# A causal long convolution with a gated feed-forward on one core: block 2's spectrum by n mod 4, two product sums by accumulating transfers, and a new order of the work

## The chip, the cores and the metric

One Trainium2 chip, one of its cores. The metric is device time in microseconds of one execution, from inputs in HBM to the output in HBM; the times given are medians of several runs. The core's engines are named as in the profile: PE (TensorE) multiplies matrices, DVE (VectorE) and ACT (ScalarE) work on elements, POOL (GpSimd) does small element work and issues transfers, SP only issues transfers. Each takes its own instructions strictly in order and waits where a semaphore makes it wait.

## The reference

For one sequence of 2048 positions with 640 channels (A_q, A_k, A_v are 2048 x 640):

```python
k_shift = sum(k_pad[:, t:t+S] * shift_k[:, 3-t] for t in range(4))   # causal filter of 4 taps along the sequence
kv = k_shift * v
y  = irfft(rfft(pad(kv)) * rfft(pad(ssm_k)))[:S]                     # causal convolution over all 2048 positions, by channel
y  = y + kv * ssm_D
h  = x + layernorm(x) * y                                            # x = A_q
h2 = h + (silu(layernorm(h) @ w_gate) * (layernorm(h) @ w_up)) @ w_down   # 640 -> 1728 -> 640
```

Inputs and output are bfloat16. B_x is not used.

## The kernel before

**Blocks.** The sequence is cut into four blocks of 512 positions. A block lies as 128 partitions x 4 residues r = n mod 4 x 640 channels. Block j of the convolution needs inputs 0 to j with kernel slices j to 0: each input block and each slice gets a spectrum of its own once, the products are summed over the pairs, and one inverse transform gives the block. The transform is an odd-frequency DFT of length 1024, done as matmuls with constant matrices: `WF` forward, `WI` inverse. A spectrum is a tile `S` of two halves in frequency, each with two cosine and two sine rows of 640 channels (128 x 2560 elements a half).

**Stages of block j**, with the names that the code gives its steps: loads (`Lg`, `Lk`, `Lv`, `Lx`); `g`: the kernel slice turned; `G`: its spectrum; `h`: windows of neighbouring slices; `k`: the 4-tap filter on PE and the product with v; `X`: the spectrum of the input; `m0`..`m3`: products of spectra; `n`: sums for the first layernorm; `i`: inverse transform, h and the sums of the second layernorm; `t`: layernorm of h, turned for the feed-forward; `f`: the feed-forward (13.5 chunks of 128 gate and up columns, then the down projection). The feed-forward of block j - 1 runs on PE among the convolution steps of block j; that of block 3 has nothing left beside it.

**Order.** The program first writes down all steps as a plan, each with an engine, what it reads and writes, and the buffers it holds. `ORDER` is a list of the plan's numbers, written out by hand or by a tool: the program is issued in that order, so each engine's queue is the list filtered by its engine. A negative number ~n takes step n's second form: an eviction from PSUM or an application of a layernorm on DVE in place of ACT, or a weight load issued by POOL in place of SP. Buffers (12 of `big`, 8 of `S`, 4 of PSUM and so on) go in turn to the steps as they come in the list; a step that takes a buffer waits for the last user of it.

**Spectrum, two forms** (`transform`, L391). In the form "sub" each of the four basis rows is summed by PE over residues 0 and 2, evicted doubled, then over 1 and 3 on top, evicted; DVE's one difference of full half-size (128 x 2560) gives the second half of the frequencies. In the form "four" PE sums each of the cosine and sine rows over one residue, then over a second, for even and for odd residues:

```python
forward(src, 2 * sin, rs[:1], ps, ws, True, False, [odd, dst])
taken(ps, tmp[1], tmp[0], ws, True)
forward(src, 2 * sin, rs[1:], ps, ws, False, True, [odd, dst])
taken(ps, a[1], a[0], ws)
```

DVE then makes one difference of 128 x 1280 for the even and one for the odd residues, `hi4` (full size) is the upper half, and the lower half is a sum that, for the names in `ADDLO` ('G1', 'G2', 'X1', 'X2', 'X3'), is not made by DVE: `add_into` (L276 to L279) lets POOL issue a transfer from SBUF to SBUF that adds to its target. `SUM` names the transforms that take the form "four".

**Products** (`mac`, L707). For each pair of spectra after the first, four steps: a product (L746) and its sum into `A` (L747) on DVE. Where the pair of parts stands in `ADDP` under (block, input), the step is a product alone (L741), and the sum into `A` is an accumulating transfer by `add_into`. The products of block 3 with inputs 1 and 2 are the steps `m1`, `m2` of that block.

**Inverse** (`inverse`, L813). In the form "four" (blocks 2 and 3) DVE makes two half-size steps for the even residues (L843) and two for the odd ones (L858); then PE makes one product for each residue (L878). The sum of A's halves ahead of it is an accumulating transfer in block 2. POOL makes the scale of the second layernorm in blocks 1 and 2 (`norm`, L760 to L791).

Of the kernel before, what the change touches and what calls it, by code (L numbers as in the profile page):

```python
# [46 lines left out]
SUM = {'X3': 'four', 'i2': 'four', 'i3': 'four', 'G3': 'four'}  # L47
ADDP = {(1, 1): ((0, 1),)}
# [164 lines left out]
def kernel(ctx: ExitStack, tc: tile.TileContext, A_q, A_k, A_v, A_shift_k, A_ssm_k, A_ssm_D, B_x,  # L213
# [165 lines left out]
    def wide(n, ws):  # L379
        return n if len(ws) == 2 else n // 2 + 75  # L380
# [10 lines left out]
    def transform(src, dst, pieces, minus=None, name=None):  # L391

        how = SUM.get(name, "sub")
        for ws in pieces:
# [418 lines left out]
    def inverse(A, x, n1, pieces=((0, 1),), minus=None, groups=(ROWS,)):  # L813
# [4 lines left out]
        for ws in pieces:  # L818
            if not minus:
# [10 lines left out]
                else:  # L830
                    dve(wide(1490, ws), low, [], [(A, bits(ws=ws))])
            four = not minus and SUM.get(f"i{plan.block}") == "four"
            if four:
# [404 lines left out]
    for j in range(1, NB):  # L1238
# [25 lines left out]
        if last:  # L1264
            A = H[j]
            stage("m0")
            mac(A, X[0], H[j], True, at=(j, 0), adds=ADDP.get((j, 0), ()))
        stage("k")
# [62 lines left out]
```

## Time and profile before

| | |
|---|---|
| time, median of 3 runs | 260.67 us (260.61 to 261.63) |
| the profiled execution's own time | 261.3 us |
| its span, first to last instruction | 259.6 us |
| PE busy | 251.3 us (97%) |
| DVE busy | 198.6 us (77%) |
| ACT busy | 180.0 us (69%) |
| POOL busy | 97.0 us (37%) |
| DMA | 45.38 MB, mean 175 GB/s |

Times in the profile are microseconds from the span's start, or ns where a column says mean of one. A busy share is an average over the whole span; the stages have different limits, so the table of stretches says more. In a row of a timeline stand start, duration, engine, line of the kernel, operation, target <- sources, and in brackets how long the engine sat idle before it and what ended that. Matmuls overlap in PE's pipeline, so the duration of one (299 ns at 320 columns) is longer than the distance to the next.

### The profile page before, as it was taken

What the parts mean: (1) busy time and instruction counts of PE and PEld (TensorE: products, weight loads), DVE (VectorE), ACT (ScalarE), POOL (GpSimd) and SP (SyncE); (2) the same over time, 40 slices, a digit from 0 to 9 for tenths busy, and PEclk for the clock granted to TensorE, in tenths of its full rate; (3) what the DMA queues carried; (4) which work ended last, traced back from release to release, by engine and by line L of the source; (5) the groups of instructions that cost most, each with busy time, mean ns of one, the idle gap of its engine ahead of it and who ended that gap; (6) DMA issues with size and microseconds to landing.
All of it is one profiled execution on the core that took longest, in us unless ns stands there. A gap on an engine that the chain in (4) does not pass through costs nothing.

```text
span 259.6 us, 4700 instructions
## 1 busy us (share of the span) xinstructions
PE 251.3 (97%) x1803; PEld 154.2 (59%) x1818; DVE 198.6 (77%) x259; ACT 180.0 (69%) x297; POOL 97.0 (37%) x115
## 2 busy tenths in 40 slices
PE   8999899999998999999999999999999999999994
PEld 7967577654654477754465477544456764444663
DVE  4679999999998999999999999999998200004403
ACT  2899999999998998569855985655497134637200
POOL 7961300008914199926117962240951022000000
PEclk9999999999999999999999999999999999999999
DMA  6997999979999998999997965994498546000002
GB/s 218 403 251 119 289 252 340 280 115 279 247 238 168 182 217 204 190 191 201 214 231 110 299 151 107 198 238 130 100 215 255 101 77 70 8 0 0 13 15 76
DMA packets 64752, 45.38 MB, mean 175 GB/s; under 512 B 31014, under 2 KB 60267, under 8 KB 64731
## 3 DMA queue, kind: packets, MB, share of 16 engines
q1 hardware_dynamic: 58896, 32.96, 51.1%
q0 software_dynamic: 5824, 12.13, 24.9%
q8 instruction: 14, 0.23, 0.4%
q14 instruction: 8, 0.06, 0.1%
q10 hardware_dynamic: 10, 0.01, 0.0%
HBM read 30.01 MB, written 4.59 MB: 133 GB/s over the span
## 4 chain that ended last, share of the span: by engine, by line
PE 78%; ACT 9%; DMA 6%; DVE 2%; issue 2%; SPq 1%; ACTq 0%; DVEq 0%
PE ps L1022 40%; PE ps L1110 23%; PE ps L375 10%; DMA big<-in_B_w_up_dram 4%; PE ps L878 3%; DMA big<-in_A_q_dram 3%; ACT T L565 2%; ACT big L364 1%; ACT S L364 1%; PE ps L648 1%; ACT row L757 1%; ACT big L664 1%; ACT big L473 1%; ACT tT L1014 1%; DVE row L892 1%
## 5 line engine op out<-in xcount | busy, mean ns | idle before, releaser
L1022 PE MATMUL ps<-big,big 128*128 128x512 bf16 x525 | 119.9, 379 | 1.7 <-DMA big<-in_B_w_up_dram 0.8
L1022 PEld LDWEIGHTS <-big 128*128 128x128 bf16 x540 | 52.5, 98 | 61.1 <-DMA big<-in_B_w_up_dram 1.3
L1110 PE MATMUL ps<-wd,tT 128*128 128x320 bf16 (+1 forms) x416 | 60.3, 299 | 0.0
L1110 PEld LDWEIGHTS <-tT 128*128 128x128 bf16 x416 | 40.7, 98 | 16.3
L1016 DVE TENSOR_TENSOR tT<-tT,co 128x2048 bf16<-128x2048 bf16 x12 | 14.5, 1219 | 34.4 <-ACT tT L1014 32.4
L375 PE MATMUL ps<-big,WF 128*128 128x320 bf16 x240 | 39.1, 299 | 1.3 <-ACT big L364 1.0
L1012 ACT CAST co<-ps 128x1024 bf16<-128x1024 f32 x24 | 24.2, 1011 | 17.3 <-PE ps L1022 16.8
L747 DVE TENSOR_TENSOR S<-S,big 128x2560 bf16<-128x2560 bf16 x23 | 34.3, 1492 | 1.2 <-DMA S<-big 0.5
L746 DVE TENSOR_TENSOR big<-S,S 128x2560 bf16<-128x2560 bf16 x23 | 34.1, 1485 | 0.2
L375 PEld LDWEIGHTS <-WF 128*128 128x128 bf16 x240 | 23.1, 97 | 12.8 <-issue 2.3
L1014 ACT ACTIVATE tT<-ps 128x1024 bf16<-128x1024 f32 x24 | 24.5, 1029 | 8.8 <-PE ps L1022 8.7
L757 ACT ACTIVATE row<-big 128x640 bf16<-128x640 bf16 x32 | 23.5, 742 | 1.8 <-DMA big<-in_A_q_dram 1.1
L807 ACT ACTIVATE row<-big,sm 128x640 bf16<-128x640 bf16 x23 | 20.3, 922 | 3.8 <-POOL sm L789 2.8
L1117 POOL DMA_DIRECT2D out_dram<-row x12 | 11.8, 1010 | 29.2 <-ACT row L1116 29.1
L364 ACT CAST S<-ps 128x320 bf16<-128x320 f32 (+1 forms) x36 | 19.4, 583 | 0.3
L1116 ACT CAST row<-ps 128x640 bf16<-128x640 f32 x12 | 8.1, 691 | 14.2 <-PE ps L1110 13.2
L364 ACT ACTIVATE big<-ps 128x640 bf16<-128x640 f32 (+1 forms) x24 | 15.6, 696 | 0.7 <-PE ps L375 0.7
L278 POOL DMA_DIRECT2D big<-row x8 | 7.0, 919 | 22.9 <-DVE row L892 22.9
L892 DVE SCALAR_TENSOR_TENSOR row<-row,ps 128x640 bf16<-128x640 bf16 x16 | 12.8, 815 | 1.1 <-PE ps L878 0.9
L278 POOL DMA_DIRECT2D S<-big x2 | 2.5, 1266 | 26.3 <-DVE S L719 19.1
L719 DVE TENSOR_TENSOR big<-S,S 128x2560 bf16<-128x2560 bf16 (+1 forms) x10 | 12.2, 1218 | 0.1
L959 POOL DMA_DIRECT2D big<-in_B_w_gate_dram x8 | 9.1, 1137 | 8.1 <-PE ps L1022 7.8
(110 smaller groups left out, 330.4 us busy)
## 6 DMA issues: line engine op xcount, KB each, us to landing
big<-in_B_w_up_dram SPq DMA_DIRECT2D x17, 320.0 KB, 5.1
big<-in_B_w_gate_dram SPq DMA_DIRECT2D x16, 320.0 KB, 4.7
big<-in_A_ssm_k_dram SPq DMA_DIRECT2D x4, 640.0 KB, 9.2
big<-in_A_q_dram SPq DMA_DIRECT2D x4, 640.0 KB, 7.6
big<-in_A_v_dram SPq DMA_DIRECT2D x4, 640.0 KB, 6.9
big<-in_B_w_gate_dram POOLq DMA_DIRECT2D x8, 320.0 KB, 7.2
big<-in_B_w_up_dram POOLq DMA_DIRECT2D x7, 320.0 KB, 6.7
wd<-in_B_w_down_dram SPq DMA_DIRECT2D x1, 2080.0 KB, 12.2
```

The costliest lines, as they stand in the source:

```text
L364: (lambda: nc.scalar.activation(dst(), src(), ACT.Copy, scale=2.0)) if twice else (lambda: nc.scalar.copy(dst(), src())),
L375: nc.tensor.matmul(ap(ps)[:, h, 0:NH], w, ap(src)[:, r, h * NH:(h + 1) * NH], start=(first and i == 0), stop=(last and i == len(rs) - 1), ...
L746: nc.vector.tensor_mul(flat2(b), X.part(xs), H.part(hs))
L747: f(A.part(dst), A.part(dst), flat2(b))
L757: act(825, lambda r=r, junk=junk: nc.scalar.activation(ap(junk), ap(x)[:, r, :], ACT.Square, scale=D ** -0.5, accum_out=sm(s, 1)[:, r:r + ...
L807: nc.scalar.activation(ap(row), ap(x)[:, r, :], ACT.Identity, bias=sm(s, 5)[:, r:r + 1], scale=sm(s, 4)[:, r:r + 1])
L892: nc.vector.scalar_tensor_tensor(two(ap(t)), two(ap(t)), 1.0, half(ap(ps)), op0=ALU.mult, op1=ALU.mult, accum_out=sm(s, 0)[:, r:r + 1])
L1012: act(1010, lambda ps=ps: nc.scalar.copy(ap(co)[:, at:at + 2, :], ap(ps)), src, [(co, gi % 2)])
L1014: act(1010, lambda ps=ps: nc.scalar.activation(ap(tT)[:, c:c + 2, :], ap(ps), ACT.Silu), src, [done(range(c, c + 2), ROWS)])
L1016: dve(1220, lambda: nc.vector.tensor_mul(ap(tT)[:, c - 2:c + 2, :], ap(tT)[:, c - 2:c + 2, :], ap(co)), [co], [done(range(c - 2, c + 2), R ...
L1022: nc.tensor.matmul(ap(ps)[:, i, :], ap(w)[:, k, off:off + P], ap(hT)[:, k, :], start=(k == 0), stop=(k == KT - 1))
L1110: nc.tensor.matmul(ap(ps)[:, hf, to:to + n], t, ap(wd)[:, c, col + (hf - hs[0]) * NH:col + (hf - hs[0]) * NH + n], start=(c == order[0]), ...
```

## The change

Three constants:

- `SUM` gets 'X2': 'four': the spectrum of input block 2 is made in the form "four". PE's matmuls for it go from 32 to 16, its evictions stay eight; DVE gets two differences of 128 x 1280 and keeps one of 128 x 2560; since 'X2' is in `ADDLO` already, its lower half is an accumulating transfer.
- `ADDP` gets (3, 1) and (3, 2) with the pair (0, 1): in block 3 the product of the cosine part of inputs 1 and 2 with the sine part of their windows is added to the result by an accumulating transfer instead of by DVE.
- `ORDER` is another list: 919 numbers in place of 914 (three more for the spectrum, one more for each of the two products).

```diff
-SUM = {'X3': 'four', 'i2': 'four', 'i3': 'four', 'G3': 'four'}
-ADDP = {(1, 1): ((0, 1),)}
+SUM = {'X3': 'four', 'i2': 'four', 'i3': 'four', 'G3': 'four', 'X2': 'four'}
+ADDP = {(1, 1): ((0, 1),), (3, 1): ((0, 1),), (3, 2): ((0, 1),)}
 ADDINV = (2,)
...
 ORDER = [
-    0, 2, 31, 1, 4, 5, 7, 10, 6, 8, 16, 13, 12, 11, 22, 29, 26, 37, 27, 14, 3, 15, 23, 28, 42, -39, 9, 35, -37, 24, 39, 205, 40,
...
+    1, 4, 0, 2, 22, 31, 29, 27, 13, 5, 7, 6, 9, 10, 14, 35, 39, 26, 16, 3, 15, 33, 28, -37, -41, 42, 34, 37, 41, 38, 12, 61, 11,
...
```

Numbers up to 447 mean the same steps in both lists; 448 to 467 are block 2's spectrum in the new plan (448 to 464 before); behind it the new number is the old one plus 3, plus 4 from the first and plus 5 from the second new transfer on. Read with that, the new list differs from the old in these places:

- Front: v of block 0 (27) is loaded ahead of x (26). The four transposing loads of block 1's keys (197 to 200) stand ahead of the load of its kernel slice (192) on SP. ACT copies the first filtered keys (44) ahead of the sums of the first layernorm. DVE makes the products of block 0 for the first half of the channels as soon as that half's spectra are there, and the second half among the inverse's steps. Ten evictions of input 0's spectrum are on DVE instead of eight.
- First feed-forward: PE's first product (344) has four more matmul steps of G2 ahead of it; the odd chunk that reads the weights of load 368 (step 374) stands 8.7 us of PE work later.
- Block 1 and 2: the transfer for the lower half of X2 (467) stands on POOL behind block 1's normalisation (304) and one weight load (527); between X2's difference (466) and the products of block 2 with it (478 to 481) stand two products with sums, one half-size step of G3 and two small products of the feed-forward on DVE.
- Block 2's inverse: PE's first step is that of residue 1 (497) instead of residue 2.
- Block 3: its products come in the order (0,1) of input 1 first, then those that do not need the result of the transfer; the same for input 2, with two products of input 3 ahead of the last.
- Feed-forward weights: 19 of their loads are issued by POOL instead of 15; layernorm of h in block 3 is four steps on DVE instead of three on DVE and one on ACT, and in block 2 four on ACT instead of three.

71 rows, old and new, of the table ORDER are left out of this document.

## The prediction

> **What bounds the kernel now.** I read the page first, then the busy time in 20 stretches of 13 us (their columns: PE, its weight loads, DVE, ACT, POOL, then granted clock, DMA share and GB/s), then the chain that ended last, then TensorE's (PE's) timeline around the only data wait in that chain.
>
> ```profile
> PE 251.3 (97%) x1803; PEld 154.2 (59%) x1818; DVE 198.6 (77%) x259; ACT 180.0 (69%) x297; POOL 97.0 (37%) x115
> 117.00:130.00 13.00, 12.95 (x65) 5.94 (x64) 12.91 (x13) 12.10 (x12) 4.70 (x5) 1.00 1.05 210
> 182.00:195.00 13.00, 12.95 (x67) 6.38 (x66) 12.62 (x16) 9.42 (x11) 9.88 (x10) 1.00 0.68 168
> 208.00:221.00 13.00, 12.95 (x71) 6.86 (x70) 0.00 (x0) 4.61 (x6) 3.47 (x4) 1.00 0.54 75
> 71.61 9.45 DMA big<-in_B_w_up_dram
> 81.11 0.39 PE ps L1022
> 130.01 0.66 PE ps L648 x20
> 130.67 1.08 PE ps L1022 x5
> 240.84 15.23 PE ps L1110 x112
> 79.08 1.24 PE L1022 MATMUL ps<-big,big 128*128 128x512 bf16 x5
> 81.11 1.25 PE L1022 MATMUL ps<-big,big 128*128 128x512 bf16 x4 [0.78 <-DMA big<-in_B_w_up_dram]
> ```
>
> PE is busy nearly everywhere at full granted clock (the 1.00 in the stretches), so matmuls taken away shorten the kernel as long as PE keeps being fed. But VectorE (DVE) is as full as PE, 12.91 and 12.62 of 13 us, until it has nothing left after 208. In the convolution stages the two run side by side: PE fills the time with the feed-forward products of the block before, while DVE makes the spectral products from which the next block's products come. What counts is at which handovers DVE delivers later than PE arrives. PE itself loses time for data once: the five matmuls at 79.08 are issued in 1.08, the next starts at 81.11, so 0.95 us are lost to a weight load.
>
> The profiled execution took 261.3 us with a span of 259.6; the 1.7 us around the span I leave as they are. The median of the timed runs is 260.67, so I work out a difference on the profiled execution and apply it to 260.67. About 0.5% (1.3 us) is what a measurement of this kernel can tell from no change.
>
> **1. Block 2's spectrum by n mod 4.**
>
> ```profile
> L375 PE MATMUL ps<-big,WF 128*128 128x320 bf16 x240 | 39.1, 299 | 1.3 <-ACT big L364 1.0 <-ACT big L473 0.2
> ```
>
> These are the spectra's matmuls. The old form makes 32 matmuls of 320 columns (four basis rows, four residues, two halves of the width), the new one 16, since each basis row is summed over two residues instead of four. Their 299 ns are the latency of one in the pipeline; the last 112 of this width take 15.23 us, so 0.136 each: 16 x 0.136 = **-2.18 us of PE work**. The eight evictions stay eight. DVE gets two differences of half size more; its full-size difference stays, and the full-size sum is not DVE's: it goes to an accumulating transfer.
>
> **2. The accumulating transfers.** Three more: the low half of block 2's spectrum, and the cosine-by-sine products of inputs 1 and 2 in block 3.
>
> ```profile
> L747 DVE TENSOR_TENSOR S<-S,big 128x2560 bf16<-128x2560 bf16 x23 | 34.3, 1492 | 1.2 <-DMA S<-big 0.5
> L746 DVE TENSOR_TENSOR big<-S,S 128x2560 bf16<-128x2560 bf16 x23 | 34.1, 1485 | 0.2
> L535 DVE TENSOR_TENSOR S<-big,S 128x1280 bf16<-128x1280 bf16 x4 | 3.1, 815 | 0.0
> L1016 DVE TENSOR_TENSOR tT<-tT,co 128x2048 bf16<-128x2048 bf16 x12 | 14.5, 1219 | 34.4 <-ACT tT L1014 32.4
> L1034 DVE TENSOR_TENSOR tT<-tT,co 128x512 bf16<-128x512 bf16 x4 | 1.7, 422 | 1.0 <-ACT co L1033 0.9
> 118.92 1.48 DVE L823 TENSOR_TENSOR big<-S 128x2560 bf16<-128x2560 bf16 x1
> 120.71 1.24 POOL L278 DMA_DIRECT2D S<-S x1 [1.60 <-DVE big L823]
> 129.51 1.55 DVE L843 TENSOR_TENSOR S<-S 128x1280 bf16<-128x1280 bf16 x2
> S<-big POOLq DMA_DIRECT2D x2, 640.0 KB, 8.3
> L278 POOL DMA_DIRECT2D S<-big x2: 1250/1266/1283, 59.5 to 160.8; - x2
> DMA to landing us min/median/max: 6.8/8.8/9.9
> L278 POOL DMA_DIRECT2D S<-big x1: 1250/1250/1250, 160.8 to 160.8; - x1
> DMA to landing us min/median/max: 6.8/6.8/6.8
> ```
>
> DVE's books: minus two full-size sums (2 x 1.49), plus two half-size differences (2 x 0.82), plus three more evictions handed to DVE (about 0.4 each): nearly nothing. So the change frees PE, not DVE.
>
> The four transfers of this size in the trace landed 6.8 to 9.9 us after issue (the two into S from big: 8.3), and the issue followed DVE's result by 0.3 us (118.92 + 1.48 to 120.71). What covers them is the DVE work that the new order puts between result and use. For the two product sums that is 10.5 and 10.2 us (for the latter three products with sums, 2.98 a pair, and the product of the next, at the closer spacing of below): more than 0.3 + 9.9, so they are hidden. If the cover fails they cost what DVE then waits. Their three issues take 3 x 1.27 on POOL; behind the first stands block 2's normalisation, still due in time.
>
> For the low half of block 2's spectrum the cover is thin. Between its difference and block 2's products with it stand two products with sums (2 x 2.98), one half-size step (0.82) and two products of the feed-forward tail (2 x 0.42): 7.6 us by durations. Starts follow each other closer than that (two steps of 0.82 in 1.55 at 129.51), so 7.2. **DVE waits 0.3 + 8.3 - 7.2 = 1.4 us**; with 6.8 it is nothing, with 9.9 it is 3.0. The low half of block 3's spectrum, which already goes this way, gets the same thin cover in the new order (two products with sums and a product), but its transfer, the one at 160.8, landed in 6.8, and by the same count as in part 5 PE has over 1 us in hand after it: 0 taken, 1 at the other end.
>
> [...]
>
> **3. The new order, front.** Block 0's stage decides how far DVE is behind.
>
> ```profile
> 1.72 7.11 DMA big<-in_A_q_dram
> L337 SPq DMA_DIRECT2D big<-in_A_v_dram x1: 432/432/432, 2.9 to 2.9; - x1
> DMA to landing us min/median/max: 7.6/7.6/7.6
> 8.34 4.63 PE L639 MATMUL ps<-big,T 128*128 128x128 bf16 x80
> 8.85 0.74 ACT L757 ACTIVATE row<-big 128x640 bf16<-128x640 bf16 x1 [1.07 <-DMA big<-in_A_q_dram]
> 11.03 0.67 ACT L664 CAST big<-ps 128x640 bf16<-128x640 f32 x1
> 22.50 0.82 DVE L719 TENSOR_TENSOR S<-S,S 128x1280 bf16<-128x1280 bf16 x1
> ```
>
> Now x lands first (8.83), v at 10.5, and ScalarE (ACT) does three layernorm sums before its first copy of a shifted-key product, at 11.03. That product was there after a quarter of the 4.63 us, at 9.5. The new order loads v first and puts the copy first, so this copy can start 1.5 us earlier; besides, the spectral products (22.50) no longer wait for both halves of the width. I take DVE as **1.6 us less late** from here. It costs something: the load of the next kernel slice moves behind four transposing loads on SP. If it comes late it holds PE, and the gain is gone: 0 at the other end, 2.0 at best. For PE itself I take nothing: 2.2 us more of other matmuls stand ahead of the first feed-forward product, and ACT, which must bring the last transposed rows first, is full there either way.
>
> **4. The data wait at 81 us.** The product that waited stands 8.7 us of PE work later in the new order, and the weights' buffers come free no later. **-0.95 us**; 0 if the wait reappears.
>
> **5. Where DVE catches PE: block 2's inverse.**
>
> ```profile
> 132.27 0.71 PE L878 MATMUL ps<-S,WI 128*128 128x320 bf16 x4
> 83.48 0.82 DVE L892 SCALAR_TENSOR_TENSOR row<-row,ps 128x640 bf16<-128x640 bf16 x1 [0.72 <-PE ps L878]
> 201.71 5.17 SPq L919 DMA_TRANSPOSE big<-row  x4
> big<-row SPq DMA_TRANSPOSE x12, 2.6
> 211.53 0.81 PE L1022 MATMUL ps<-big,big 128*128 128x512 bf16 x2
> ```
>
> Before, the first matmul of this inverse starts at 132.27 and needs the first of the two steps at 129.51, done at 130.33: 1.9 us in hand. The new order starts the inverse with an odd residue, which needs three more half-size steps. Ahead of them stand also the two new differences and one more step of block 3's kernel window, but no longer one product of the feed-forward (L1016), and DVE has the three evictions more: 6 x 0.74 - 1.14 + 1.2 = +4.5 us. From this go the 1.6 of part 3, and 0.7 because DVE no longer waits at 83 for the matmuls held by the weights. DVE is ready at 130.33 + 4.5 - 1.6 - 0.7 + 1.4 = 133.9. PE has two feed-forward products (2 x 1.08) and one shifted-key product (0.66) more in front, 2.18 less from part 1: it arrives at 132.27 + 0.6 - 0.95 = 131.9. So **PE waits 2.0 us** here; with the transfer hidden 0.6.
>
> **6. The end.** The last four transposing transfers are issued from 201.71 to 206.88 and land 2.6 after the last issue began (205.65), at about 208.3; the last block's feed-forward starts at about 211.5, so 3 us are in hand. DVE's whole work ahead of these transfers is 0.35 us more and it is about 1 less late, while PE arrives 1 us sooner: still 2 in hand. The tail (the sum with the residual and the last store) is as before.
>
> Sum: -2.18 - 0.95 + 2.0 = **-1.1 us**: span 258.5, own time 260.2, median **259.6 us**.
>
> **Rivals.** (a) *The transfer is hidden* (it lands in 6.8 as at 160.8): PE waits 0.6, -2.5 us, **258.2**; with an early gain of 2.0 it is 257.8. For it: the last transfer of this size. Against: the other three took longer, up to 9.9. [...]
>
> (b) *Nothing is gained in front*, since the late kernel slice holds PE, or the transfer takes 9.9: either adds 1.6 us to the wait of part 5, and the sum is +0.5, **261.2**. For it: the transfers near 100 us run beside four transposing transfers, two weight loads and a 640 KB load.
>
> (c) *Slower: POOL reaches the issue late.* On POOL the new transfer stands behind block 1's normalisation and one weight load.
>
> ```profile
> 90.52 0.90 POOL L959 DMA_DIRECT2D big<-in_B_w_gate_dram  x1 [5.05 <-PE ps L1022]
> 91.50 1.39 POOL L766 TENSOR_SCALAR sm<-sm 128x4 f32<-128x4 f32 x1
> 100.10 0.47 POOL L789 TENSOR_TENSOR sm<-sm 128x4 f32<-128x4 f32 x1
> ```
>
> The normalisation took from 91.50 to 100.57, after a weight load had held POOL for 5.05 us. In the new order the buffer of the last load ahead of it is freed by products that PE reaches near 86, some 4 us sooner, so POOL should be at the issue by 99, when DVE's difference is also ready. If it is held as before, the issue comes at 102 or later; from 2.5 us of delay on the kernel is slower by over 0.5%, and with 3.5 the sum is -1.1 + 3.5 = +2.4, **263.1**. Against it: nothing new stands ahead of the normalisation but that one load.
>
> **How the numbers follow.** Chances: the forecast 0.40, (a) 0.22, (b) 0.23, (c) 0.15. The range 257.7 to 262.3 takes in (a), (b), the bounds of parts 2 to 4, and the beginning of (c). The forecast's own scatter (the wait between 0.7 and 2.7) reaches from 258.9 to 260.3 around 259.6; its faster end and (a) make 0.45 for faster by over 0.5%, (c) and the slow end of (b) 0.21 for slower, 0.34 between.
>
> **What would show it.** Right: 240 recorded matmuls of the spectra's line become 224; three more accumulating issues on POOL; no data wait of the up-projection weights near 80 us; an idle time of DVE ahead of a product of block 2 that ends with the landing of a transfer into S; an idle time of PE before the first inverse matmul of block 2, released by DVE; the first products of block 0 on DVE before 21.5 us. Wrong: PE waits elsewhere, above all in front of the kernel-slice transposes at 24 us or of block 3's feed-forward; or the landing of the three transfers takes longer than 10 us, since three more transfers slow each other.

## The result, and the profile after

The changed kernel is **slower**: 268.63 us (median of six runs, 266.33 to 269.90) against 261.15 for the kernel before on the same chip (260.57 to 262.07), a ratio of 1.0282 with a 95% interval of 1.0231 to 1.0334. Forecast was 259.6. The profiled execution took 268.76 us with a span of 267.0, before 261.3 and 259.6. Ratios here and below leave out runs more than 1.5% above the fastest of the same kernel; medians and ranges are over all runs.

The page after, first the engines, then the groups of TensorE (PE), then the transfers:

```profile
PE 252.5 (95%) x1786; PEld 154.6 (58%) x1802; DVE 199.9 (75%) x263; ACT 178.3 (67%) x294; POOL 97.1 (36%) x122
...
L1023 PE MATMUL ps<-big,big 128*128 128x512 bf16 x524 | 120.0, 381 | 4.6 <-DMA big<-row 3.4
...
L376 PE MATMUL ps<-big,WF 128*128 128x320 bf16 x224 | 36.9, 301 | 1.5 <-ACT big L365 1.2
...
S<-big POOLq DMA_DIRECT2D x5, 640.0 KB, 7.2
```

The 16 matmuls are gone (240 to 224) and three accumulating transfers have come. But PE is busy for 252.5 us where it was 251.3, with less work, and its idle time in front of the feed-forward products has grown. Three of the 13 us stretches show where (PE, its weight loads, DVE, ACT, POOL, then granted clock, DMA share, GB/s):

```profile
104.00:117.00 13.00, 9.42 (x63) 6.16 (x62) 11.02 (x9) 6.01 (x9) 3.64 (x5) 0.92 1.01 165
117.00:130.00 13.00, 12.95 (x63) 6.39 (x63) 10.62 (x10) 9.88 (x13) 6.94 (x9) 0.95 0.93 219
156.00:169.00 13.00, 11.39 (x85) 8.07 (x84) 11.10 (x11) 8.07 (x14) 6.71 (x5) 1.00 0.75 168
```

PE and DVE both lose there, and the granted clock falls to 0.92 and 0.95 in the first two. The chain of waits into the first hole:

```profile
100.81 0.56 POOL sm L790
101.38 1.73 ACT row L808 x2
...
105.46 0.58 ACT row L1117
106.05 0.25 SPq L920
106.35 3.25 SPq L920
109.69 5.59 DMA big<-row
...
115.41 0.58 PE ps L1023
```

Block 1's normalisation ends on POOL, ACT applies it to four rows, SP issues four transposing loads of these rows. One issue takes 3.25 us, the last load lands 5.59 after its issue, at 115.28; only then can block 1's feed-forward start. PE's timeline, DVE's at the same place, POOL's and PE's at the second hole, and the end:

```profile
111.35 0.71 PE L376 MATMUL ps<-big,WF 128*128 128x320 bf16 x4
...
115.41 0.58 PE L1023 MATMUL ps<-big,big 128*128 128x512 bf16 x1 [3.35 <-DMA big<-row]
...
101.33 1.49 DVE L444 TENSOR_TENSOR S<-S,big 128x2560 bf16<-128x2560 bf16 x1
...
111.92 1.49 DVE L747 TENSOR_TENSOR big<-S,S 128x2560 bf16<-128x2560 bf16 x1 [1.85 <-DMA S<-big]
...
151.54 1.26 POOL L279 DMA_DIRECT2D S<-big  x1 [0.33 <-DVE big L742]
...
160.99 1.14 POOL L790 TENSOR_TENSOR sm<-sm 128x4 f32<-128x4 f32 x1
...
166.15 3.69 PE L1111 MATMUL ps<-wd,tT 128*128 128x320 bf16 x26 [1.61 <-ACT big L365]
...
262.82 1.03 PE L1111 MATMUL ps<-wd,tT 128*128 128x256 bf16 x8 [0.65 <-DVE row L1128]
```

Adding up, step by step, the time from the end of one PE step to the end of the next, the changed kernel's PE ends 7.9 us later (263.96 against 256.05): +1.8 up to the turned rows of block 0, +0.5 in block 0's feed-forward and block 2's input, **-1.9 in block 2's spectrum**, **+7.0 in block 1's feed-forward and block 3's window spectrum beside it**, -0.3 after it, +0.8 in the last block's feed-forward.

### The profile page after: what moved, and what is told of

Same layout as the page of the kernel before. It is cut to its first block, busy times and chain, and to the rows that moved or that the text cites. A ratio compares the mean times of both kernels' runs of the same rounds, so it can differ in the third digit from the quotient of the medians.

```text
span 267.0 us, 4657 instructions
## 1 busy us (share of the span) xinstructions
PE 252.5 (95%) x1786; PEld 154.6 (58%) x1802; DVE 199.9 (75%) x263; ACT 178.3 (67%) x294; POOL 97.1 (36%) x122
## 4 chain that ended last, share of the span: by engine, by line
PE 54%; DVE 16%; ACT 9%; POOL 8%; DMA 7%; issue 4%; SPq 1%; DVEq 0%; POOLq 0%
PE ps L1023 31%; PE ps L1111 14%; DVE S L720 5%; DMA S<-big 4%; ACT row L808 2%; ACT row L758 2%; DMA big<-row 2%; DVE big L720 2%; PE ps L879 2%; PE ps L376 2%; POOL sm L788 2%; PE ps L640 2%; DVE row L893 2%; ACT big L365 1%; SPq L920 1%
## 5 line engine op out<-in xcount | busy, mean ns | idle before, releaser
L1111 PE MATMUL ps<-wd,tT 128*128 128x320 bf16 (+2 forms) x416 | 60.4, 299 | 2.3 <-ACT big L365 1.6
L376 PE MATMUL ps<-big,WF 128*128 128x320 bf16 x224 | 36.9, 301 | 1.5 <-ACT big L365 1.2
L747 DVE TENSOR_TENSOR big<-S,S 128x2560 bf16<-128x2560 bf16 x21 | 31.2, 1485 | 4.4 <-PE ps L1023 2.5
L748 DVE TENSOR_TENSOR S<-S,big 128x2560 bf16<-128x2560 bf16 x21 | 31.3, 1492 | 0.7
L376 PEld LDWEIGHTS <-WF 128*128 128x128 bf16 x224 | 21.8, 98 | 13.4 <-issue 3.2
L365 ACT CAST S<-ps 128x320 bf16<-128x320 f32 (+1 forms) x32 | 17.7, 600 | 0.9 <-PE ps L376 0.7
L960 POOL DMA_DIRECT2D big<-in_B_w_gate_dram x11 | 11.1, 1011 | 10.5 <-PE ps L376 3.5
L365 ACT ACTIVATE big<-ps 128x640 bf16<-128x640 f32 (+1 forms) x18 | 12.0, 704 | 3.7 <-PE ps L376 2.5
L279 POOL DMA_DIRECT2D S<-big x5 | 6.3, 1261 | 19.4 <-DVE S L720 9.2
```

The costliest lines, as they stand in the source:

```text
L365: (lambda: nc.scalar.activation(dst(), src(), ACT.Copy, scale=2.0)) if twice else (lambda: nc.scalar.copy(dst(), src())),
L376: nc.tensor.matmul(ap(ps)[:, h, 0:NH], w, ap(src)[:, r, h * NH:(h + 1) * NH], start=(first and i == 0), stop=(last and i == len(rs) - 1), ...
L747: nc.vector.tensor_mul(flat2(b), X.part(xs), H.part(hs))
L748: f(A.part(dst), A.part(dst), flat2(b))
L1111: nc.tensor.matmul(ap(ps)[:, hf, to:to + n], t, ap(wd)[:, c, col + (hf - hs[0]) * NH:col + (hf - hs[0]) * NH + n], start=(c == order[0]), ...
```

## The experiments

Three theories stood at first. **T**: the low half's transfer slows the transposing loads that fly beside it. **O**: the order itself makes the rows late. **S**: the first product sum of block 3 stands in front of block 2's normalisation. Four kernels undo the parts one by one in the new order.

**Old spectrum in the new order.**

```
-SUM = {..., 'G3': 'four', 'X2': 'four'}
+SUM = {..., 'G3': 'four'}
 ORDER: block 2's spectrum steps in the old form, at the same places
```

> The changed kernel with block 2's spectrum in its old form (32 matmuls, one difference of full size on DVE, no accumulating transfer of the low half); the two transfers of block 3 and the new order stay. Theory T (the low half's transfer flies beside the four transposing loads of block 1's normalised rows, so that these land late, PE waits 3.4 us for them and then runs 3.4 us at half the granted clock, which costs 1.7 more): all of that goes, 2.2 us of PE work come back, 268.6 - 5.1 + 2.2 = 265.7; the transposing loads land in about 5 us instead of 7.5. Theory O (the order alone makes the rows late: block 1's normalisation ends later and the feed-forward is reached sooner): PE arrives 2.2 later, so 1.2 of wait stay and with them a shorter stretch of half clock; the loads land as late as in the changed kernel; 268.6 +- 1.

Measured: 266.39 us (265.89 to 269.02), ratio 1.0187 (1.0132 to 1.0242). The four loads land in 2.6 to 2.7 us, PE has no data wait in front of block 1's feed-forward, and the mean granted clock of the profiled execution is 0.997. T's number was 265.7.

**No product sums as transfers.**

```
-ADDP = {(1, 1): ((0, 1),), (3, 1): ((0, 1),), (3, 2): ((0, 1),)}
+ADDP = {(1, 1): ((0, 1),),}
```

> The changed kernel with the two product sums of block 3 back on DVE (two sums of 1.49 us there, no accumulating transfers for them); the rest stays. Theory S (the first of these transfers stands on POOL ahead of block 2's normalisation and makes its rows late, for which PE waits about 2 us before block 2's feed-forward): that wait goes and 268.6 - 2.0 = 266.6. Theories T and O: block 2's rows are late because DVE and PE are late since block 1; the wait stays, DVE has 3 us more to do, 268.6 to 270.

Measured: 267.49 us (266.46 to 269.11), 1.0215 (1.0171 to 1.0259). S's half: the wait in front of the down projection at the second hole falls from 1.6 to 0.8. The first hole stays in another shape: ACT waits 3.85 us for the row loads, and PE 3.02 for ACT.

**The order alone**, both edits above at once.

> The new order alone: block 2's spectrum in the old form and both sums of block 3 on DVE. T and S together: 268.6 - 5.1 + 2.2 - 2.0 = 263.7. O: the order itself costs what was seen, and without its saving of 2.2 us of PE work it is 268 to 271.

Measured: 264.82 us (264.73 to 269.08), **1.0107** (1.0074 to 1.0141), nearer to T and S together than to O, yet not 1.00. The costs add: order 1.07%, sums 0.80% (1.0187 less 1.0107), spectrum 1.08% (1.0215 less 1.0107), together 2.95 where 2.82 was measured. The intervals of the kernel with the sums and of the order alone overlap, so the sums' term is not clear of noise; the intervals behind the spectrum's term do not overlap. The spectrum that frees 2.2 us of PE *costs* 2.8. The transposing loads' line (duration of an issue min/median/max, first and last start; then issue to landing) of the changed kernel, of the kernel without sums, of the order alone, and of the kernel before shows T's mechanism:

```profile
L920 SPq DMA_TRANSPOSE big<-row x4: 1213/1562/3253, 103.1 to 109.7; - x4
...
DMA to landing us min/median/max: 5.6/7.5/8.4
```

```profile
L920 SPq DMA_TRANSPOSE big<-row x4: 1217/1710/2572, 104.5 to 111.0; - x4
...
DMA to landing us min/median/max: 2.6/3.8/5.8
```

```profile
L920 SPq DMA_TRANSPOSE big<-row x4: 1199/1220/1269, 103.3 to 107.5; - x4
...
DMA to landing us min/median/max: 2.6/2.6/2.7
```

```profile
L919 SPq DMA_TRANSPOSE big<-row x4: 1198/1260/1439, 101.6 to 106.8; - x4
...
DMA to landing us min/median/max: 4.0/4.8/4.9
```

The transfer was issued at 103.38 and landed 8.3 later, so the loads flew beside it. In the order alone each lands in 2.6 to 2.7 and SP issues one in 1.2. In the kernel before, which has no transfer there, they landed in 4.0 to 4.9: the transfer is not the only thing that can slow them.

**DVE sums the low half**, no transfer, all else as changed.

```
-ADDLO = ('G1', 'G2', 'X1', 'X2', 'X3')
+ADDLO = ('G1', 'G2', 'X1', 'X3')
```

> The changed kernel with block 2's spectrum by n mod 4, but its low half summed by DVE (1.49 us) instead of by an accumulating transfer; the rest stays. T: the row loads of block 1 land in about 5 us, PE waits under 0.5 us before block 1's feed-forward and keeps its full clock, DVE loses 1.5 and gains the 1.9 that it waited for the transfer and the 2.2 that it waited for PE: 268.6 - 5.1 = 263.5. O: the wait before block 1's feed-forward stays at 3 us or more, 268 to 270.

Measured: 268.12 us (264.50 to 269.23), 1.0150 (1.0078 to 1.0221): against T's number. T's first half holds (the row loads land in 2.7 to 4.5, the last at 108.9), but another load takes the place of the wait in the profiled execution (268.87 us; the ratio rests on runs of 264.50 and 267.37). DVE's and SP's timeline:

```profile
106.64 1.49 DVE L747 TENSOR_TENSOR big<-S,S 128x2560 bf16<-128x2560 bf16 x1 [4.85 <-DMA big<-big]
...
93.12 7.86 SPq L462 DMA_TRANSPOSE big<-big  x1
```

The last turned row of block 3's window kernel, queued on SP behind three other loads, took 7.86 us to issue; DVE's next product writes the buffer that it reads. Two kernels move only this load up, behind its three sisters, one with DVE's low sum, one with the transfer.

```
 ORDER: the fourth transposing load of block 3's window kernel
        right behind the third, ahead of the weight and kernel loads
```

> As the changed kernel with DVE's low sum, and the last of the four transposing loads of block 3's window kernel issued on SP right behind the other three, ahead of three weight and kernel loads. Where that load stood behind them it took 7.9 us to issue and landed 13.4 us after; the buffer it reads is the one that DVE's next product writes, and DVE waited 4.85 us, PE 3.5 behind DVE, with a stretch at half clock after it. Theory Q (that is the whole cost of the variant): 268.1 - 3.5 - 1.7 = 262.9, within 1. Rival (the loads now behind it are late in turn, or the junction before block 1's feed-forward is bound by block 1's normalisation whatever one does): 265 to 268.

> The changed kernel with only the last transposing load of block 3's window kernel moved up on SP behind the other three; the transfer of the low half stays. The same with DVE's low sum measured 1.016. Theory T (the transfer is what costs: the row loads beside it land in 5 to 8 us instead of 2.6): 1.023 to 1.029, and they land so late again. Rival (the late turned row was the cost, not the transfer): 1.013 to 1.018, the row loads land in 3 to 4.

Measured: with DVE's sum 265.34 us (264.38 to 265.76), **1.0160** (1.0121 to 1.0200), 2.4 us above Q's number and in the rival's range; with the transfer 268.94 (268.25 to 269.18), **1.0297** (1.0239 to 1.0355), the upper end of T's range. The row loads with DVE's sum, then with the transfer, where they land late again:

```profile
L920 SPq DMA_TRANSPOSE big<-row x4: 1207/1242/1272, 105.0 to 109.1; - x4
...
DMA to landing us min/median/max: 2.6/2.7/4.0
```

```profile
L920 SPq DMA_TRANSPOSE big<-row x4: 1256/1732/2899, 103.6 to 110.1; - x4
...
DMA to landing us min/median/max: 5.2/6.9/7.8
```

So the two differ only in who sums the low half, and that is worth 1.4%: T is shown. With its own sum DVE comes to the products with X2 even 0.5 us later (111.88 against 111.42); what goes is PE's wait of 2.96 us for the row loads, and the mean granted clock is 0.999 where it was 0.990.

**Block 2's spectrum in the old order**, once with the transfer, once with DVE's sum.

```
 ORDER of before; spectrum by n mod 4; the low half's transfer behind
 its difference, one product of input 1 moved behind it
```

> The kernel before, with its order, and only block 2's spectrum by n mod 4 with the accumulating transfer of the low half (issued right behind its difference; one product with its sum of input 1 moved behind it, so that about 6 us of DVE work cover it). Theory P (the part costs what it cost in the new order, 2.7 us there between the kernel without sums and the order alone: the transfer slows the transposing loads of block 1's rows beside it, PE reaches the feed-forward sooner and waits): 261.8 + 2.7 = 264.5, these loads land 6 to 8 us after issue instead of 4 to 4.9, PE waits 2 to 4 us in front of or near block 1's feed-forward. Theory O (the part is sound and only the new order spoils it): the 2.2 us of PE come through, less a DVE wait of 2: 259.6 to 261.

```
 ORDER of before; spectrum by n mod 4; the low half summed by DVE
```

> The kernel before, in its own order, with only block 2's spectrum by n mod 4 and the low half summed by DVE: no transfer, no buffer held longer. PE has 2.2 us less to do, DVE 3.1 us more ahead of block 2's inverse, where PE had 1.9 in hand. Theory V: PE waits 1 to 3 us at or behind this inverse and nothing is gained, 0.999 to 1.010 of before. Rival: PE is the bound and the 2.2 come through, 0.990 to 0.995.

Measured with the transfer: 271.94 us (266.48 to 277.44), 1.0232 (1.0184 to 1.0280) from its runs of 266.48 and 267.30 us: more than P's number, and far from O's. The profiled execution is the one of 277.44; it shows a third way to pay, in SP's timeline and the chain:

```profile
114.80 0.37 SPq L960 DMA_DIRECT2D big<-in_B_w_up_dram  x1
115.27 2.69 SPq L920 DMA_TRANSPOSE big<-row  x2
```

```profile
116.62 11.27 DMA big<-row
...
128.03 2.29 PE ps L1023 x5
```

The last two row loads stood on SP behind a weight load that did not issue before 114.80, and then landed 11.27 after issue. The transfer holds a buffer of the pool that weights share; that this is what the weight load waited for is only argued, and whether the two faster runs paid in the same way no trace shows.

Measured with DVE's sum: 263.04 us (262.67 to 263.70), **1.0086** (1.0060 to 1.0112): V's number, not the rival's. So in the old order too the transfer (there with one product moved to cover it) costs 1.5% more than DVE's sum. This kernel's row loads, one group of PE's waits, and PE's timeline:

```profile
L920 SPq DMA_TRANSPOSE big<-row x4: 1199/1572/2511, 101.1 to 107.6; - x4
...
DMA to landing us min/median/max: 5.9/6.2/6.4
...
PE ps L376 <- ACT S L365: 1.1, 2, 0.7
...
113.73 2.54 PE L1023 MATMUL ps<-big,big 128*128 128x512 bf16 x10
...
133.56 0.72 PE L879 MATMUL ps<-S,WI 128*128 128x320 bf16 x4 [0.60 <-DVE S L844]
...
137.91 1.25 PE L879 MATMUL ps<-S,WI 128*128 128x320 bf16 x8 [0.82 <-DVE row L893]
```

Block 1's feed-forward starts at 113.73 where it started at 113.66 before: of 2.2 us saved nothing arrives. PE waited 1.1 us inside the shortened spectrum (0.36 at 93.70 and 0.73 at 96.81, none there before) for ACT to empty its PSUM tiles, and 0.41 at 109.88 for another copy by ACT, which had itself waited 2.2 for a row load. At block 2's inverse PE now waits for DVE, 1.4 us. V named only this second place. The row loads were as late as 6.4 us here without any new transfer, but PE did not wait for them in front of the feed-forward.

**No transfer at all in the new order**, and the same mended.

```
 ORDER: DVE's low sum, early turned row, sums of block 3 on DVE
```

> New order, block 2's spectrum by n mod 4 with its low half summed by DVE, both sums of block 3 on DVE, and the last transposing load of block 3's window kernel issued right behind the other three: no accumulating transfer of the change is left. Beside the order alone (1.0107) it has 2.2 us less of PE work and 3.1 more of DVE's. Theory V (DVE sets the pace in blocks 1 and 2, so PE's saving comes back as waits): 1.008 to 1.012. Rival (PE's saving counts once the transfer is gone): 1.000 to 1.004.

Measured: 264.18 us (263.76 to 265.20), 1.0112 (1.0065 to 1.0158), as the order alone has with 2.2 us more of PE work: V's number again. In the profiled executions block 1's feed-forward does start 2.5 us sooner than in the order alone (110.83 against 113.37), block 2's still 1.9 and the last block's 0.95; the saving is lost on the way.

**The order mended** in three places, with the old spectrum and with the new.

```
 ORDER: last kv product of block 2 ahead of input 0's products;
        one feed-forward product of block 0 two products later;
        last block's down projections in the old sequence
```

> The new order alone (old spectrum, sums on DVE), mended in three places where its profile showed a wait that the kernel before has not: the last product of block 2's kv (0.48 us on DVE) ahead of the products of X0 with H2, since PE waited 1.0 for it; one feed-forward product of block 0 (1.2 us on DVE) two products later, since DVE waited 1.2 for ScalarE there; and the last block's down projections in the old sequence, since the two last pieces of a row share a PSUM tile and PE waited 0.65 for DVE between them. Theory M (the order alone costs 1.07% through these places): 1.0 + 0.8 less on PE, 0.998 to 1.005 of before. Rival (behind each stands another wait of the same chain, DVE's lateness at block 2's inverse above all): 1.007 to 1.011, only the tail's 0.3% gained.

> The one before, with the three places mended as in the mended order. M: 0.6% less than that kernel has, 0.999 to 1.006. Rival as there: only the tail's 0.3%, 1.005 to 1.009.

Measured: 263.62 us (263.00 to 265.41), 1.0108 (1.0072 to 1.0144), and 265.09 (263.40 to 266.61), 1.0134 (1.0061 to 1.0208). The tail's 0.8 us is gone in both profiles, the wait for kv too, and the time is the same. In the first, PE now waits 1.6 in front of block 1's kv (`PE ps L649 <- DMA T<-T`), which the profiled execution of the order alone did not show. That is not the mending's doing: the profiles of six other kernels with this front show the same wait, 0.4 to 1.3 us, and that of the filled one below 2.8. The rival holds for the first; the second is too wide to say more than that nothing was gained.

**Old front, new front.** Both without the two parts, joined where the two orders have done the same steps but seven.

```
 ORDER: steps 1-350 of before, then the new order / steps 1-349 of
        the new order, then that of before
```

> Old spectrum, sums on DVE; the first 350 steps in the order before (up to the products of input 1 with the window of block 0, about 64 us), the rest in the new order. Beside the kernel before 1.0 and the new order alone 1.0107. Theory F (the front of the new order makes everything behind it late: spectra of blocks 0 and 1 cost PE 2.4 us more there): 1.000 to 1.005. Rival G (the rest does: block 2's rows 3.5 us later and the last block's down projections 0.8): 1.007 to 1.012.

> Old spectrum, sums on DVE; the first 349 steps in the new order, the rest in the order before. Theory F: 1.005 to 1.010. Rival G: 0.998 to 1.003.

Measured: old front 268.60 us (268.05 to 269.91), 1.0301 (1.0226 to 1.0375): nobody's number. The join itself made PE wait 3.1 for ACT in front of block 2's kv, with a granted clock of 0.50 after it (75.97 to 79.38), so it tells nothing of the order. New front: 264.33 (261.23 to 266.61), 1.0090 (1.0046 to 1.0135), as F said; behind the join its PE steps take what they took before. The new front alone thus costs about as much as the whole order. Its profiled execution waits at one place most, in front of block 1's kv, and that of the mended order at the same line for another load:

```profile
PE ps L649 <- DMA big<-in_B_w_up_dram: 2.1, 1, 2.1
```

Since one half of the pair is spoilt and this one scatters over 5 us, the pair supports F and does not show it. The other traces add to it: block 0's feed-forward starts at 49.64 to 49.81 us in all five profiled executions with the old front, and at 52.76 to 56.85 in all 13 with the new one. The 16 matmuls more that stand ahead of it explain 2.2 of that, so the new front made PE 0.9 to 5.0 us late in every one of them.

**One sum of two.**

```
-ADDP = {..., (3, 1): ((0, 1),), (3, 2): ((0, 1),)}
+ADDP = {..., (3, 2): ((0, 1),)}
 (DVE's low sum and early turned row as above)
```

> As the variant with DVE's low sum and the early turned row, and only the second of the two product sums of block 3 as a transfer (the first, which stands on POOL ahead of block 2's normalisation, is back on DVE). Both sums as transfers measured 1.016, none 1.0112. Theory S (it is the first one that costs, by making block 2's rows late): 1.010 to 1.013, and PE's wait in front of block 2's feed-forward is under 1 us. Rival (the second costs as much, or neither does): 1.014 to 1.017.

Measured: 264.81 us (261.99 to 265.06), 1.0118 (1.0043 to 1.0194), and the wait at the second hole is 0.80 instead of 1.61. These are S's numbers, but the interval also holds the rival's.

**Both sums in the old order.**

```
 ORDER of before; each sum's transfer behind its product, the
 products of block 3 in the changed kernel's sequence
```

> The kernel before, with its order, and only the two product sums of block 3 as accumulating transfers; the products of block 3 are put in the changed kernel's sequence (cosine by cosine and sine by sine first), so that 6 to 12 us cover each. Theory P (the part costs what it cost in the new order, 1.6 us, of which 0.8 is a longer wait in front of block 2's feed-forward): 262.6 to 263.4. Rival (hidden, and DVE has 3 us less to do late in its work, where PE has time in hand): 261.8 within 0.4.

Measured: 273.74 us (272.81 to 275.65), 1.0504 (1.0452 to 1.0557), far from both. POOL's and DVE's timeline:

```profile
149.86 1.28 POOL L279 DMA_DIRECT2D S<-big  x1 [0.34 <-issue]
...
143.52 1.49 DVE L742 TENSOR_TENSOR big<-S,S 128x2560 bf16<-128x2560 bf16 x1
...
155.94 1.49 DVE L747 TENSOR_TENSOR big<-S,S 128x2560 bf16<-128x2560 bf16 x1 [10.94 <-DMA S<-big]
```

The product was done at 145.01, but its transfer stood behind the normalisation on POOL until 149.86, and the very next product, which does not read the sum, waited for its landing; that it writes the buffer which the transfer still reads is inferred from this wait. So my placing was measured here and not the part; it suggests why the changed kernel puts this transfer ahead of the normalisation.

**The wait filled.**

```
+FILL = {549: 48}      # 48 matmuls of 128 columns on a constant,
+                      # ahead of block 1's first feed-forward product
```

> The changed kernel with 48 matmuls of 128 columns on a constant in front of the first product of block 1's feed-forward (2.7 us of PE work into a PSUM tile that the product then overwrites), where PE waited 3.6 us for the transposing loads. Theory H (the half clock of 3.4 us after the wait costs 1.7 us in most runs): the granted clock stays at 1.00 there, 268.6 - 1.7 = 266.9 or the 266.3 that the changed kernel's fastest run showed, with little scatter. Rival (block 1's feed-forward is not what sets the end there, since DVE is as late): 268.6, unchanged.

Measured: 268.04 us (266.11 to 275.02), 1.0251 (1.0197 to 1.0306): inconclusive. The profiled execution is the one of 275.02. There PE waited 3.8 us in front of the spectrum ahead of the filler, and 2.8 for a transfer (T<-T) up to 37.73 us. The granted clock was 0.50 from 39.17 to 42.58, after the second; its mean of 0.988 over 273.3 us makes 6.6 us at half clock in all (an estimate), so about as much lies elsewhere, by my reading behind the first wait. If so, the filler came too late.

## Why the prediction was wrong

The sum was -1.1 us; measured are +7.5. By its steps:

**Part 1, the 16 matmuls: right in size, wrong in worth.** -2.18 forecast, -1.9 measured in the spectrum's steps. But the first sentence of the argument, that matmuls taken away shorten the kernel as long as PE is fed, failed. With DVE's sum in the old order block 1's feed-forward started at 113.73 instead of 113.66, and PE waited 1.4 us more at block 2's inverse. "The eight evictions stay eight" was true, but it was put at nothing: with half the matmuls PE came for the next PSUM tile before ACT had emptied it, and waited 1.1 us inside the spectrum itself. PE was 97% busy, and yet ACT and DVE were ready only just in time for it.

**Part 2, the transfers: the step that failed.** The landing was right to the tenth (8.3), by luck, since 8.3 was the middle of 6.8 and 9.9 and later transfers of this kind landed in 5.7 to 7.2. DVE's wait was nearly right (1.85 for 1.4; the issue followed the result by 0.56 us, not 0.3), and the two product sums were hidden, as forecast. What was left out is what flies beside it: I costed the transfer only against its own reader. The four transposing loads landed 5.6 to 8.4 us after issue, where they took 4.0 to 4.9 before and 2.6 to 2.7 in the new order without the transfer; PE waited 3.35 us for them, and the granted clock was 0.50 from 114.94 to 118.35. Rival (b) even names transfers beside transposing loads, but prices only the transfer's landing, not theirs. The transfer against DVE's sum is 1.4%, 3.6 us (268.94 to 265.34). The profile of the kernel before could have warned: 2.6 is the median of all twelve such loads, and just these four took 4.0 to 4.9, beside other transfers.

**Part 2, "behind the first stands block 2's normalisation, still due in time": wrong.** It ended at 152.5 before and at 162.1 now, 9.6 later (157.9 in the order alone, so over half of this is not the transfers'); PE's start of block 2's feed-forward, which needs its rows, moved by 7.1. In front of it ACT waited for the normalisation, an eviction of block 3's spectrum stood behind ACT's row steps, and PE's down projection needed its PSUM tile: 1.61 us. The wait is half as long in the kernels without the first sum.

**Part 3, the front: right at its first step, wrong in what it gains.** The first product of block 0 on DVE came at 21.83 in this execution, not before 21.5, against 22.50 before. That was a slow start: PE's small matmuls stayed slow for longer (16 of 128 columns took 1.84 us at 7.50 here, 1.10 at 6.56 before), and between 5.41 and 9.12 us it did 38 of them instead of 67.

```profile
5.41:9.12 3.71, 3.71 (x38) 3.71 (x37) 2.55 (x13) 1.47 (x3) 1.69 (x4) 1.00 1.02 376
...
10.01 1.28 PE L640 MATMUL ps<-big,T 128*128 128x128 bf16 x20
```

(The records of the granted clock begin at 9.12 in this execution, at 5.41 before; ahead of the first record the view prints 1.00.) The shifted-key product thus began at 10.01, 1.7 later than before, whatever v did. In ten of the other twelve profiled executions with this front the first product came at 19.91 to 21.02, as forecast, and in two at 21.76 and 21.94. But the lead was not kept: by the first inverse step DVE was at 35.53 here and at 33.60 to 35.64 in the others, against 34.28, so never 1.6 earlier. And PE, for which nothing was taken, lost 2.3 us in the front here, as the start of block 0's feed-forward shows (54.18 against 49.70, less 2.2 for the 16 matmuls).

**Part 4: right.** The wait near 80 us is gone. **Part 5: overtaken.** PE began block 2's inverse at 140.41 instead of the 133.9 forecast and did not wait there, where 2.0 was forecast, as it was late itself: DVE's half-size steps were done at 139.41. **Part 6: half right.** The last block's feed-forward began without a wait; "the tail is as before" was wrong by 0.8 us, since two pieces of a row now share a PSUM tile back to back and PE waits 0.65 for DVE between them.

**Rival (c)** had the right sign and a condition that came true (issue at 102 or later; it was 103.38), but by another way: DVE's difference was done only at 102.82, so POOL was not late. The list of what would be wrong did name PE waiting in front of another feed-forward, for block 3; it was block 1.

What stays open: which steps of the new order alone lose its 1%. In its profiled execution PE is 0.9 us late at block 0's feed-forward (after the 2.2 for the 16 matmuls), 2.8 at block 2's, 3.1 at the last block's and 3.9 at its end; it starts late in every execution with the new front, but the pair that should have shown the front to be the cause did not. No version tried beats the kernel before.

## What to carry to other kernels

Price a transfer against everything that flies beside it, not only against its reader: look for the loads that the next handover waits for, and give the sum to an engine if its time is shorter than their delay. Before counting work taken off the busiest engine as gained, follow the next handover back: if the other side was ready only just in time, the saving can turn into a wait, as 2.2 us of PE work did here with DVE's sum in the old order. And ask what stands around an asynchronous sum in its queue and who needs its buffer: in the old order with both sums its issue stood behind the normalisation on POOL until 149.86, and DVE waited 10.94 us for its landing.

## What the runs showed of the hardware

**The granted clock was 0.50 for 3.41 us at a time, and not only after an idle PE.** In the changed kernel it is 0.50 for exactly one stretch of 3.41 us, from 114.94 to 118.35, which follows a stretch of the same length in which PE was busy 0.54 us. Three matmuls of 512 columns took 1.48 us in it (at 116.22), five took 1.24 behind it (at 119.01). The busy times by stretches of this length, cut at the bounds shown, of the changed kernel, of the filled one and of the one without sums (PE first, the granted clock behind POOL):

```profile
111.52:114.94 3.42, 0.54 (x4) 0.17 (x2) 2.99 (x3) 0.77 (x2) 0.00 (x0) 1.00 1.09 233
114.94:118.35 3.41, 2.71 (x8) 1.22 (x10) 3.38 (x3) 1.81 (x3) 2.49 (x4) 0.50 0.67 194
```

```profile
35.76:39.17 3.41, 1.45 (x43) 1.45 (x44) 1.50 (x5) 0.56 (x1) 0.00 (x0) 1.00 1.07 189
39.17:42.58 3.41, 3.41 (x49) 2.84 (x46) 2.26 (x5) 2.35 (x6) 0.22 (x1) 0.50 0.94 257
```

```profile
106.96:110.38 3.42, 1.52 (x10) 0.97 (x10) 2.95 (x3) 0.47 (x1) 0.00 (x0) 1.00 1.11 179
110.38:113.79 3.41, 1.77 (x14) 1.27 (x14) 2.80 (x2) 1.72 (x3) 1.51 (x2) 1.00 0.82 145
```

1.45 us of 3.41 (0.42) was followed by half clock, 1.52 (0.45) was not. The length of a wait does not settle it: two waits of 1.0 and 3.0 us (106.53 to 107.49 and 109.00 to 112.02) left 1.52 and 1.77 us busy in two stretches and cost no clock, while a wait of 2.8 (34.95 to 37.73), also spread over two, left 1.45 in the second, and half clock followed. That the busy time within one such stretch is what counts is my reading of these three executions, which no run tests. A stretch of 3.41 us at half clock costs 1.7, an estimate (half of 3.41). That fits the changed kernel's scatter: the run at a mean granted clock of 0.999 took 266.33, the five at 0.986 to 0.994 took 268.43 to 269.90. It is not the whole of it: with the early turned row and the transfer, the run at 1.000 was the slowest of four, 269.18.

**One small step of POOL took 1.45 us beside a working DVE and 0.20 beside a waiting one.** One step of the same normalisation, 128x4 elements, in the kernel before (DVE working) and in the old order with both sums (DVE waiting from 145.0 to 155.9):

```profile
147.80 1.45 POOL L785 TENSOR_TENSOR sm<-sm 128x4 f32<-128x4 f32 x1
```

```profile
147.61 0.20 POOL L786 TENSOR_TENSOR sm<-sm 128x4 f32<-128x4 f32 x1 [1.95 <-ACT row L758]
```

1.45 us against 0.20. The seven steps of the normalisation took 8.8 us in the first and 3.6 in the second, of which 1.5 was the one step that DVE was still working beside. That DVE's work is the cause rests on this comparison alone.
